# A fused attention and GEGLU block on one core: GpSimd's queue given out by a modelled clock, tangents, differences and projections held for smaller counted backlogs of ScalarE, no filler matmuls in three-tile steps

## The chip, the cores and the metric

The kernel runs on one core of one Trainium2 chip. The metric is the device time of one execution in microseconds. The core has TensorE (PE), VectorE (DVE), ScalarE (ACT), GpSimd (POOL) and SyncE (SP, which here only issues DMAs). Each engine takes its own instructions in order; they wait for each other with semaphores.

## The reference

The input x has 2048 rows of 512 values (bfloat16). The block is a pre-norm transformer layer with 32 heads of 16 values and a gated FFN of 1792 hidden values:

```python
h  = x + A(layernorm(x))      # A: qkv = x @ wqkv; 32 heads, Dh = 16; softmax(q k^T / 4) v; @ wo
h2 = h + B(layernorm(h))      # B: (gelu_tanh(x @ w_gate) * (x @ w_up)) @ w_down
```

## The kernel before

**Units and steps.** The attention is cut into 64 units: eight groups of 256 rows, and in each group eight slots of four heads. A unit is 16 steps, p0 to p15, so the program counts 1024 steps ("ticks"). In a step, two passes run side by side. Pass 1 (`p1_pair`, L825) computes the scores of 128 rows against 512 keys for two heads into two PSUM banks, and VectorE takes their row maxima in one instruction (L840). When a unit's maxima are there, GpSimd combines them to the negative row maximum, split into three bfloat16 parts (L868 to L876), a DMA transposes them (STG), and GpSimd adds them to three spare rows of Q (L888, function `add`), so that the scores of pass 2 come out with the maximum already subtracted. Pass 2 follows 24 steps behind: two tiles a step, each of two matmuls (L904) into one of four rotating banks and one exponential on ScalarE (L933) into a ring of probability tiles. At p7 to p10 of the unit after next, the PV matmuls (L947, sixteen a step) use those tiles; the result is evicted to OB at p10 (L669), transposed by DMA, and normalised by GpSimd (L981, a power of -1, and L985).

**Joint units.** In eleven units (`JOINT`: 12, 14, 17, 20, 25, 28, 33, 36, 41, 44, 49) one step's pair of scores is left out: ScalarE writes two *differences* of scores beforehand (`item_diff`, L1027, after GpSimd has negated a part of Q, L1014), and VectorE takes one combined maximum per head (L837, two instructions instead of one L840). Step p14 of such a unit is skipped; pass 2 makes up its two tiles in p15 of that unit and p1 of the next, which then have three tiles (`more`). The run has 1013 executed steps.

**The dense stream.** The remaining work is a queue of items that `Dense.piece` starts between the steps: Q, K and V projections in the first units; then for each group the output projection (`item_oproj`: L1087, L1091, eviction with row sums L1094, and two steps or more later the squares L1101, then the layer norm on GpSimd and a transposing DMA, hnT); the FFN's gate and up products (L1168), seven of each, with evictions to g_sb and u_sb (L669); and two down projections (`item_down`, L1220, L1225). Gelu is done in pieces: GpSimd computes the polynomial (L1158, L1159, L1160), ScalarE the tangent (L1148), GpSimd the rest (L1156, L1157) and the product with the up half (L1212, GUT). An item uses two buffers in turn, so a gate waits for the product of the one before the last. The list `prio` (PV, output projections) comes ahead of `ready` (gate, up, down); `extra` holds the differences. A step in which no item ran gets two filler matmuls of 128x512 (`want`, `dummy`, L1380).

**Two counters order the work.** They are arithmetic of the program, not measurements:

- `act_lag` is ScalarE's counted backlog. Each step it gains 0.478 for each exponential and loses 1.135 (never under 0); each eviction adds 0.48, a tangent 0.54, the OB eviction 0.27. A tangent may be issued (`later` in `gelu_chain`) when the count, plus 0.48 if a gate or up item is running, is at most `LAG_TH + SLOPE * n`, n being the steps it has waited, and the polynomial's end by the GpSimd clock is at most 1.3 us after the step's start. A gate or up item starts at 0.3 or less, a square is issued at 0.2 or less.
- `PoolStream` gives out GpSimd's work. `budget` gains 1.19 a step up to 1.25; an operation is issued when the budget reaches its cost (at most 1.0); the power L981 (`inv`) is kept out of p1 to p3 and p12 to p15. Beside it `pool.t` is a modelled time of GpSimd's queue (`charge`), with 1.135 us to a step.

Of the kernel before, what the change touches and what calls it, by code (L numbers as in the profile page):

```python
# [219 lines left out]
NPT_M, NPT_E, NPT_G = 23, 4, 7  # L220
NPT = NPT_M + NPT_E + NPT_G
PV_T = (15, 16, 17, 18)
ADDX = 3
LAGX = 8
PAUSE = 1
DOUBLES = 20
# [2 lines left out]
LAG_START = 0.3  # L229
LAG_OP = 0.2  # L230
TANH_LAG = 2
SLOPE = 0.02
JOINT = (12, 14, 17, 20, 25, 28, 33, 36, 41, 44, 49)
J_AT, J_GONE = 10, 14
LAG_EXTRA = 0.3
POLY = 1.3
TICK = 1.135
TOOK = {1.04: 1.13, 0.62: 0.7, 1.27: 1.26, 1.45: 1.67, 0.31: 0.4}
LAG_TH = 0.2


def bass_sequential_preLN__mha_block__geglu_ffn__prompt_kernel(nc, A_x, A_wqkv, A_wo, B_x, B_w_gate, B_w_up, B_w_down, out):
    dbg = None
    with ExitStack() as es:
# [97 lines left out]
        NU = len(units)  # L342
# [161 lines left out]
        class Banks:  # L504
            def __init__(self):
                self.free = [4, 5, 6, 7]
# [17 lines left out]
        class Dense:  # L524
# [12 lines left out]
            def add(self, genfn, *a, front=False, est=2, not_before=0):  # L537
                (self.prio if front else self.ready).append((genfn, a, est, not_before))
            def tick(self, now):
                self.now = now  # L540
                if self.pause > 0:
                    self.pause -= 1
# [9 lines left out]
            def piece(self):  # L552
                if self.single and self.pause > 0:
                    return 0
                while True:
                    if self.gen is None:
                        lim = 10 ** 9
                        for it in self.prio:
                            lim = min(lim, max(it[3], self.now))
                        self.prio.sort(key=lambda it: it[3])  # L560
                        if self.extra and self.now >= 16 * self.extra[0][1][0] + 2:
                            self._start(self.extra.pop(0))
                        elif self.prio and (not self.single or self.prio[0][3] <= self.now):
                            self._start(self.prio.pop(0))
                        elif self.extra and not tight() and act_lag[0] <= LAG_EXTRA and self.now + 2 <= lim and not (self.ready and self.ready[0][0] is item_up):
                            self._start(self.extra.pop(0))
                        elif self.ready and (not self.single or ((act_lag[0] <= (-1 if tight() else LAG_START) or force[0] or self.ready[0][0] not in (item_gate, item_up)) and startable(self.ready[0], lim - self.now) and self.ready[0][3] <= self.now and self.now + self.ready[0][2] + PAUSE - 1 <= lim)):
                            self._start(self.ready.pop(0))
                        else:
                            return 0  # L570
                    try:
                        cost = next(self.gen)
                        if isinstance(cost, tuple):
                            if self.single:
                                self.pause = cost[1]
                            if ticking[0]:
                                return 0
                            continue
                        return cost
                    except StopIteration as fin:  # L580
                        self.gen = None
                        self.done += 1
                        if self.single:
                            banks.give(self.bank)
                            self.pause = 0 if dve_free[0] else PAUSE
                        return fin.value
# [6 lines left out]
        dense = Dense()  # L593
        behind = [0]
        def tight():
            return dense.now // 16 in JOINT and dense.now % 16 >= J_GONE - 2 or bool(behind[0])

        deferred = []
        def defer(k, fn):
            deferred.append((dense.now + k, fn))  # L600
# [16 lines left out]
        class PoolStream:  # L617

            def __init__(self):
                self.q = []  # L620
                self.budget = 0.0
                self.t = 0.0
            def add(self, ops, then=None):
                for i, (cost, fn) in enumerate(ops):
                    self.q.append((cost, fn, then if i == len(ops) - 1 else None))
                if force[0] or not ticking[0]:
                    self.run(True)
            def spend(self, cost):
                self.budget -= cost
            def charge(self, took, ready=0.0):  # L630
                self.t = max(self.t, TICK * dense.now, ready) + took
                return self.t
            def run(self, flush=False):
                while self.q and (flush or self.budget >= min(self.q[0][0], 1.0) or (self.q[0][1].__name__ == 'inv' and dense.now % 16 == 0)):
                    if not flush and self.q[0][1].__name__ == 'inv' and dense.now % 16 in (1, 2, 3, 12, 13, 14, 15):
                        break
                    cost, fn, then = self.q.pop(0)
                    self.budget -= cost
                    self.charge(TOOK.get(cost, cost))
                    fn()  # L640
                    if then is not None:
                        then()
            def tick(self):
                self.budget = min(self.budget + 1.19, 1.25)
                self.run()
        ticking = [False]
        pool = PoolStream()

        act_lag = [0.0]
# [228 lines left out]
        def negm_post(ui):  # L878
            gi, slot = units[ui]
            c, hf = gi // 2, gi % 2  # L880
            par = ui % 2
            P.dma("sp", lambda e: e.dma_start_transpose(out=STG[:, par, :].rearrange("p (q s) -> p q s", q=2), in_=ST[:, par].rearrange("p q s -> p (q s)")),
                  ("stT", par), reads=[("ST", par)], writes=[("STG", par)])
            q_ap = QT[:, c, slot, 256 * hf:256 * hf + 256]
            def add():
                pool.spend(0.7)
                pool.charge(0.63, st_end[0] + 2.75)
                P.op("pool", lambda e: e.tensor_tensor(out=q_ap, in0=q_ap, in1=STG[:, par, :], op=ALU.add), reads=[("STG", par), ("qT", slot, c, hf)], writes=[("qT", slot, c, hf)])  # L888
                q_ready.add(ui)
            defer(ADDX + (ui == NU - 1), add)  # L890
        q_ready = set()
# [165 lines left out]
        def load_xres(gi):  # L1057
            assert gi < 2 or ffn_done.get(gi - 2), "dense stream too far behind (residual reuse)"
            for k in range(2):
                P.dma("sp", lambda e, k=k: e.dma_start(out=g_h(gi, k), in_=xv[:, 2 * gi + k, :]), ("xres", gi % 2, k), writes=[("h", gi % 2, k)])  # L1060

        otok_consumed = {}
        def post_onT(gi, k):
            gp = gi % 2
            if k == 0:
                load_xres(gi)
            P.dma("sp", lambda e: e.dma_start_transpose(out=OnT[:, k, :, :], in_=Otok[:, k, :]),
                  ("onT", k), reads=[("Otok", s_) for s_ in range(NSLOT)], writes=[("OH", k)])
            if k == 1:
                otok_consumed[gi] = True  # L1070
            dense.add(item_oproj, gi, k, front=True, est=3, not_before=dense.now + 5)

        hn_left = {}
        ffn_done = {}
# [60 lines left out]
        def gelu_chain(par, dE):  # L1135
# [4 lines left out]
            def later(n):  # L1140
                if not force[0] and tight():
                    defer(1, lambda: later(n))
                    return
                if not force[0] and (act_lag[0] + (0.48 if dense.gen is not None and dense.cur in (item_gate, item_up) else 0) > LAG_TH + SLOPE * n or poly_end[par] > TICK * dense.now + POLY):
                    defer(1, lambda: later(n + 1))
# [4 lines left out]
            def poly_done():  # L1150
                poly_end[par] = pool.t
                defer(TANH_LAG, lambda: later(0))
            def second():
# [229 lines left out]
        st_end = [0.0]  # L1383
        def unit_end(ui):
            pool.spend(1.8)
            st_end[0] = pool.charge(2.0, TICK * (16 * ui + 15) + 2.35)
            negm_pre(ui)
            negm_post(ui)

        p2_started = False  # L1390
        p1_next = []
        early_target = dense.done
        tick = 0
        J_ = sorted(JOINT)
        J_PREP = {max(160, 16 * (J_[i - 1] if i else 0) + 12): J_[i] for i in range(len(J_))}
        ticking[0] = True
        def next_tile():
            n = 2 * t2 - behind[0]
# [4 lines left out]
        while True:  # L1403
# [14 lines left out]
            more = 1 if behind[0] and tick % 2 else 0  # L1418
# [12 lines left out]
            act_tick(2 * p2_ok + more)  # L1431
            if p1_ok and tick in J_PREP:
                joint_prep(J_PREP[tick])
            gp1 = tick % 2
# [42 lines left out]
            if doubles[0]:  # L1477
# [3 lines left out]
                cost = 2  # L1481
            else:
                cost = dense.piece()
# [2 lines left out]
            for fn_ in early.get(tick, ()):  # L1486
                fn_()
            if p1_ok:
                want = 2
            elif tick % 2 == 0:  # L1490
                want, alone = 0, cost or 0
            else:
                want = max(0, FILL_2 - alone)
# [45 lines left out]
```

## Time and profile before

| what | value |
|---|---|
| three timed runs | 1234.58 to 1235.58 us, median 1235.29 |
| profiled execution | 1234.76 us, its span 1232.9 us |
| granted TensorE clock | 1.00 |
| first and last maximum (L840) start | 14.7 and 1179.3 us |
| L840, L933 | 1002 maxima of 1213 ns; 2000 exponentials, about 717 ns |
| fillers (L1380) | 697 matmuls |
| tangents (L1148) | 49, first at 246.5, last at 1182.8 us |

The rows of maxima overlap in part: each lasts 1.21 us, the next one starts 1.13 us after it when nothing is late. In the same way an exponential is shown with 0.72 us or more, and the next follows 0.48 us later. In the timeline, instructions of one line that follow each other closely are merged into one row with a count; the number in square brackets is the time that the engine stood idle before it, with what released it. The stages, as busy microseconds of each 100:

| window | PE | DVE | ACT | POOL |
|---|---|---|---|---|
| 100 to 200 | 85.0 | 100.0 | 98.3 | 69.1 |
| 500 to 600 | 92.1 | 98.8 | 99.95 | 63.5 |
| 800 to 900 | 91.3 | 98.9 | 99.9 | 70.2 |
| 1000 to 1100 | 87.8 | 99.7 | 98.9 | 57.9 |

After the last maximum, from about 1181 to 1204 us, ScalarE works off the exponentials that pass 2 is behind; from there to the end TensorE does the last group's output projection and FFN.

### The profile page before, as it was taken

What the parts mean: (1) busy time and instruction counts of PE and PEld (TensorE: products, weight loads), DVE (VectorE), ACT (ScalarE), POOL (GpSimd) and SP (SyncE); (2) the same over time, 40 slices, a digit from 0 to 9 for tenths busy, and PEclk for the clock granted to TensorE, in tenths of its full rate; (3) what the DMA queues carried; (4) which work ended last, traced back from release to release, by engine and by line L of the source; (5) the groups of instructions that cost most, each with busy time, mean ns of one, the idle gap of its engine ahead of it and who ended that gap; (6) DMA issues with size and microseconds to landing.
All of it is one profiled execution on the core that took longest, in us unless ns stands there. A gap on an engine that the chain in (4) does not pass through costs nothing.

```text
span 1232.9 us, 31298 instructions
## 1 busy us (share of the span) xinstructions
PE 1102.3 (89%) x12444; PEld 427.4 (35%) x12580; DVE 1179.1 (96%) x1107; ACT 1195.2 (97%) x2437; POOL 784.4 (64%) x1624
## 2 busy tenths in 40 slices
PE   7898888899999988999889998899889898888898
PEld 3233222233333333333333343333333333233335
DVE  8999999999999999999999999999999999999933
ACT  7899999999999999999999999999999999999993
POOL 8567873566756587466755677366765687347850
PEclk9999999999999999999999999999999999999999
DMA  5111113200011000100011000110001000100000
GB/s 152 27 34 30 33 50 116 76 10 9 8 27 25 8 10 9 39 13 8 11 25 27 8 8 11 25 27 8 9 10 38 14 9 8 35 17 10 8 19 14
DMA packets 68657, 31.53 MB, mean 26 GB/s; under 512 B 53920, under 2 KB 67488, under 8 KB 68512
## 3 DMA queue, kind: packets, MB, share of 16 engines
q1 hardware_dynamic: 68512, 29.52, 9.5%
q8 instruction: 101, 1.65, 0.6%
q14 instruction: 44, 0.36, 0.1%
HBM read 11.80 MB, written 2.10 MB: 11 GB/s over the span
## 4 chain that ended last, share of the span: by engine, by line
ACT 50%; DVE 30%; POOL 8%; PE 7%; issue 3%; DMA 1%; POOLq 0%; DVEq 0%
DVE PM L840 29%; ACT PTM L933 29%; ACT PTG L933 8%; ACT PTE L933 4%; PE pbank L1220 2%; ACT g_sb L669 1%; POOL th_sb L1158 1%; PE pbank L904 1%; ACT u_sb L669 1%; DMA STG<-ST 1%; PE pbank L825 1%; ACT th_sb L1148 1%; POOL LINV L981 1%; PE pbank L1168 1%; POOL GUT L1212 1%
## 5 line engine op out<-in xcount | busy, mean ns | idle before, releaser
L840 DVE TENSOR_REDUCE PM<-pbank 128x2 f32<-128x1024 f32 x1002 | 1141.4, 1213 | 8.8 <-PE pbank L904 5.1
L933 ACT ACTIVATE PTM<-pbank 128x512 bf16<-128x512 f32 x1357 | 730.3, 718 | 3.4 <-PE pbank L904 0.6
L904 PE MATMUL pbank<-QT,KT 32*128 32x256 bf16 x4096 | 512.2, 273 | 16.2 <-ACT PTM L933 6.0
L825 PE MATMUL pbank<-KT,QT 32*128 32x512 bf16 x2026 | 390.1, 384 | 29.9 <-DVE PM L840 11.3
L1380 PE MATMUL pbank<-ones_bf,ident 128*128 128x512 bf16 x697 | 217.3, 383 | 56.2 <-ACT PTM L933 29.1
L933 ACT ACTIVATE PTG<-pbank 128x512 bf16<-128x512 f32 x407 | 227.7, 716 | 1.2 <-PE pbank L904 0.2
L825 PEld LDWEIGHTS pbank<-KT,QT 32*128 32x128 bf16 x2026 | 97.7, 90 | 369.8 <-DVE PM L840 133.2
L904 PEld LDWEIGHTS pbank<-QT,KT 32*128 32x128 bf16 x4096 | 171.2, 92 | 85.2 <-ACT PTM L933 46.5
L933 ACT ACTIVATE PTE<-pbank 128x512 bf16<-128x512 f32 x236 | 139.1, 718 | 0.8
L947 PE MATMUL pbank<-PTM,VA 128*17 128x256 bf16 x2776 | 125.4, 274 | 1.5
L981 POOL TENSOR_TENSOR LINV<-OBT,negone 128x8 f32<-128x8 bf16 x62 | 103.4, 1668 | 0.0
L1380 PEld LDWEIGHTS pbank<-ones_bf,ident 128*128 128x128 bf16 x796 | 46.0, 97 | 140.1 <-ACT PTM L933 90.0
L1158 POOL TENSOR_TENSOR th_sb<-g_sb 128x512 f32<-128x512 f32 x49 | 50.9, 1040 | 41.6 <-ACT g_sb L669 41.6
L947 PEld LDWEIGHTS pbank<-PTM,VA 128*17 128x17 bf16 x2776 | 60.0, 89 | 45.7 <-issue 29.6
L1168 PE MATMUL pbank<-hnT_l,wg_sb 128*128 128x256 bf16 x448 | 67.0, 275 | 3.6
L1168 PE MATMUL pbank<-hnT_l,wu_sb 128*128 128x256 bf16 x448 | 67.1, 275 | 2.3
L868 POOL TENSOR_TENSOR MX<-PM,MX 128x8 f32<-128x8 f32 x64 | 12.8, 200 | 86.6 <-DVE PM L840 86.3
L1160 POOL TENSOR_TENSOR th_sb<-th_sb,g_sb 128x512 f32<-128x512 f32 x49 | 62.1, 1267 | 3.4
L1212 POOL TENSOR_TENSOR GUT<-th_sb,u_sb 128x512 bf16<-128x512 f32 x49 | 61.8, 1267 | 2.5
L1157 POOL TENSOR_TENSOR th_sb<-th_sb,g_sb 128x512 f32<-128x512 f32 x49 | 62.2, 1269 | 1.4
L888 POOL TENSOR_TENSOR QT<-QT,STG 128x256 bf16<-128x256 bf16 x64 | 42.7, 668 | 30.5 <-DMA STG<-ST 30.5
L1220 PE MATMUL pbank<-wd_sb,GUT 128*128 128x512 bf16 x210 | 57.3, 382 | 3.4 <-ACT OB L669 1.3
(163 smaller groups left out, 1096.0 us busy)
## 6 DMA issues: line engine op xcount, KB each, us to landing
QKS<-QKS SPq DMA_DIRECT2D x27, 112.0 KB, 2.1
x_sb<-in_A_x_dram SPq DMA_DIRECT2D x4, 512.0 KB, 5.5
xres<-in_A_x_dram SPq DMA_DIRECT2D x16, 128.0 KB, 2.3
out_dram<-out_sb SPq DMA_DIRECT2D x16, 128.0 KB, 1.7
wg_sb<-in_B_w_gate_dram SPq DMA_DIRECT2D x4, 448.0 KB, 3.6
wu_sb<-in_B_w_up_dram SPq DMA_DIRECT2D x4, 448.0 KB, 3.9
wd_sb<-in_B_w_down_dram SPq DMA_DIRECT2D x3, 512.0 KB, 4.2
STG<-ST SPq DMA_TRANSPOSE x64, 2.3
```

The source lines that it names most:

```text
L825: P.op("pe", lambda e, g=g, b=b: e.matmul(pbank[:, b, :], QT[32 * g:32 * g + 32, c, slot, 128 * qt:128 * qt + 128], KT[32 * g:32 * g + 32, ...
L840: P.op("dve", lambda e: e.tensor_reduce(out=PM[:, par, qt, kc, g:g + 2], in_=pbank[:, b:b + 2, :], axis=AX.X, op=ALU.max), reads=[("pb", b ...
L904: P.op("pe", lambda e, kt=kt, i=i: e.matmul(pbank[:, b, 256 * i:256 * i + 256], KT[32 * g:32 * g + 32, slot, 128 * kt:128 * kt + 128], QT[ ...
L933: P.op("act", lambda e, b=b, pi=pi: e.activation(out=PTt(pi), in_=pbank[:, b, :], func=ACT.Exp), reads=[("pb", b)], writes=[("PT", pi)], e ...
L947: P.op("pe", lambda e, g=g, kt=kt, pi=pi, i=i: e.matmul(pbank[32 * g:32 * g + 17, b, 0:256], VA[:, kt, 4 * slot + g, :], PTt(pi)[:, 256 * ...
L981: P.op("pool", lambda e: e.tensor_tensor(out=li, in0=o4[:, :, :, 16], in1=negone[:, 0:8].rearrange("p (q h) -> p q h", q=2), op=ALU.pow), ...
L1157: o(1.27, lambda e: e.tensor_tensor(out=ts_, in0=ts_, in1=gs, op=ALU.mult), [("th", par), ("g", par)])], then=done)
L1158: pool.add([o(1.04, lambda e: e.tensor_tensor(out=ts_, in0=gs, in1=gs, op=ALU.mult), [("g", par)], dE), o(0.62, lambda e: e.tensor_scalar( ...
L1168: P.op("pe", lambda e, dc=dc, fc=fc, i=i: e.matmul(pbank[:, b, 256 * i:256 * i + 256], w[:, dc, 128 * fc:128 * fc + 128], hT[:, dc, :], st ...
L1212: P.op("pool", lambda e: e.tensor_tensor(out=o_ap, in0=shp(ts_), in1=shp(us), op=ALU.mult), reads=[("th", par), ("u", par)], writes=o_keys ...
L1220: P.op("pe", lambda e: e.matmul(pbank[:, b, :], GUT[:, fc, 128 * k:128 * k + 128], wd_sb[:, fc, :], start=first, stop=last), reads=[("GUT" ...
L1380: P.op("pe", lambda e: e.matmul(pbank[:, b, :], ident[:], ones_bf[:, 0:512], start=True, stop=True), reads=["ident", "ones_bf"], writes=[( ...
```

## The change

It does these things:

- `PoolStream.run` no longer uses the budget. The new `fits` issues an operation when its start by the clock is at most 0.8 us (`AHEAD`) after the end of the present step, and when it doesn't run more than 0.3 us (`OVER`) past one of two due times that it would start before: the combination of maxima at the unit's end, and the addition to Q while that is outstanding (`add_due`).
- The addition to Q is put into the queue four steps after the unit's end instead of three (`ADDX`).
- Tangents: `LAG_TH` 0.05 instead of 0.2.
- Output projections: one that is due waits, for at most six steps, while the count is over 0.1, and the dense stream waits with it; the second of a group is due one step later.
- Differences: outside the last six steps before their unit they start at a count of 0.05 instead of 0.3. The first unit's preparation is at step 60 instead of 160.
- No filler in steps with three tiles.

```diff
-ADDX = 3
+ADDX = 4
+AHEAD, OVER = 0.8, 0.3
-LAG_TH = 0.2
+LAG_TH = .05
...
                         if self.extra and self.now >= 16 * self.extra[0][1][0] + 2:
                             self._start(self.extra.pop(0))
+                        elif self.prio and self.prio[0][0] is item_oproj and self.prio[0][3] <= self.now < self.prio[0][3] + 6 and act_lag[0] > 0.1:
+                            return 0
...
-                        elif self.extra and not tight() and act_lag[0] <= LAG_EXTRA and self.now + 2 <= lim and not (self.ready and self.ready[0][0] is item_up):
+                        elif self.extra and not tight() and act_lag[0] <= (LAG_EXTRA if self.now >= 16 * self.extra[0][1][0] - 6 else 0.05) and self.now + 2 <= lim and not (self.ready and self.ready[0][0] is item_up):
...
+            def fits(self, took):
+                t0 = max(self.t, TICK * dense.now)
+                if t0 > TICK * (dense.now + 1) + AHEAD:
+                    return False
+                due = [TICK * (dense.now // 16 * 16 + 15) + 2.35 if dense.now < 16 * NU else 1e9]
+                if self.add_due:
+                    due.append(st_end[0] + 2.75)
+                return not any(t0 < d < t0 + took - OVER for d in due)
             def run(self, flush=False):
-                while self.q and (flush or self.budget >= min(self.q[0][0], 1.0) or (self.q[0][1].__name__ == 'inv' and dense.now % 16 == 0)):
-                    if not flush and self.q[0][1].__name__ == 'inv' and dense.now % 16 in (1, 2, 3, 12, 13, 14, 15):
-                        break
+                while self.q and (flush or self.fits(TOOK.get(self.q[0][0], self.q[0][0]))):
                     cost, fn, then = self.q.pop(0)
-                    self.budget -= cost
                     self.charge(TOOK.get(cost, cost))
...
                 pool.charge(0.63, st_end[0] + 2.75)
+                pool.add_due = False
...
-            dense.add(item_oproj, gi, k, front=True, est=3, not_before=dense.now + 5)
+            dense.add(item_oproj, gi, k, front=True, est=3, not_before=dense.now + 5 + k)
...
             negm_post(ui)
+            pool.add_due = True
...
-        J_PREP = {max(160, 16 * (J_[i - 1] if i else 0) + 12): J_[i] for i in range(len(J_))}
+        J_PREP = {max(60, 16 * (J_[i - 1] if i else 0) + 12): J_[i] for i in range(len(J_))}
...
-                want = 2
+                want = 0 if more else 2
```

More of the change, by code (lines that the diff above doesn't have):

```diff
@@ L622, in __init__ @@
                 self.t = 0.0
+                self.add_due = False
             def add(self, ops, then=None):
@@ L643, in tick @@
             def tick(self):
-                self.budget = min(self.budget + 1.19, 1.25)
                 self.run()
```

## The prediction

> **What bounds the kernel now.** I read the page first, then the busy time by stage, then the timelines of the places where VectorE stood.
>
> ```profile
> span 1232.9 us, 31298 instructions
> ...
> PE 1102.3 (89%) x12444; PEld 427.4 (35%) x12580; DVE 1179.1 (96%) x1107; ACT 1195.2 (97%) x2437; POOL 784.4 (64%) x1624
> ...
> ACT 50%; DVE 30%; POOL 8%; PE 7%; issue 3%; DMA 1%; POOLq 0%; DVEq 0%
> ...
> L840 DVE TENSOR_REDUCE PM<-pbank 128x2 f32<-128x1024 f32 x1002 | 1141.4, 1213 | 8.8 <-PE pbank L904 5.1
> ```
>
> The profiled execution took 1234.76 us (span 1232.9), 0.5 under the median of the three timed runs, 1235.29; differences are taken from the profile and subtracted from the median. Two engines are full at once. A step of the main loop has one maximum (L840), and undisturbed maxima follow each other every 1.131 us (a row of n of them lasts n x 1.131 + 0.08). The first begins at 14.67, the last of 1013 steps at 1179.27. 1012 intervals of 1.131 are 1144.6, eleven joint steps add 0.087 each, so about 19 us were lost to waiting: 5.5 in units 0 to 2 (loads, V evictions, which the change leaves alone), nothing in units 3 to 10, and the rest later. **This rest, 13.6 us, is all that the main loop can give.** From the starts of the maxima, one by one, it falls into: 5.65 after a tangent near the PV steps; 4.46 around output projections and their squares; 1.58 at the three-tile steps; 0.33 elsewhere; 1.6 in excesses under 0.04 each, jitter. After the last maximum ScalarE works off 24 steps of exponentials (to 1203.7) and the last FFN follows (to 1232.9); no gain there.
>
> A tangent's case, unit 39, engines ACT, PE, DVE of the timeline (start, length, operation):
>
> ```profile
> 732.63 0.90 ACT L669 ACTIVATE u_sb<-pbank 128x512 f32<-128x512 f32 x1
> ...
> 734.06 0.95 ACT L1148 ACTIVATE th_sb<-th_sb 128x512 f32<-128x512 f32 x1
> ```
> ```profile
> 735.56 0.39 PE L904 MATMUL pbank<-QT,KT 32*128 32x256 bf16 x2 [0.55 <-ACT PTE L933]
> ```
> ```profile
> 729.58 6.87 DVE L840 TENSOR_REDUCE PM<-pbank 128x2 f32<-128x1024 f32 x6
> 736.86 2.35 DVE L840 TENSOR_REDUCE PM<-pbank 128x2 f32<-128x1024 f32 x2 [0.41 <-PE pbank L904]
> ```
>
> An eviction and a tangent within 1.5 us put ScalarE a whole operation behind; the score tile finds no free bank, TensorE stands 0.55, the next pair of scores is late, VectorE loses 0.41. The same tangent in unit 20, one step later in the unit and with nothing behind it:
>
> ```profile
> 392.07 0.84 ACT L1148 ACTIVATE th_sb<-th_sb 128x512 f32<-128x512 f32 x1
> ```
> ```profile
> 389.31 4.60 DVE L840 TENSOR_REDUCE PM<-pbank 128x2 f32<-128x1024 f32 x4
> ```
>
> 4 x 1.131 + 0.08 = 4.60: no loss. That pair is the core of my forecast.
>
> **Tangents (LAG_TH 0.2 to 0.05).** The code's count falls 0.179 a step: after an eviction 0.48, 0.30, 0.12, 0. Following the count through the old program, 39 of 49 tangents started above the new limit (0.05 + 0.02 per step waited); they are held one step, a few two. Of the 20 at p7, 17 stood at 0.12 or 0.16 with at most four steps waited: they go to p8 with 0, the harmless case; their stalls sum to 2.5 us. Three (units 24, 54, 62) had waited six steps: unchanged, 1.0 stays. Four at p6 of units 17, 31, 39, 47 stood at 0.30 and cost 0.49 each; held to p7 they stand at 0.12 like unit 38's, which cost 0.295: 4 x 0.2 = 0.8 gained. Held ones at p0 give 0.3, unit 22's 0.1. Sum 3.7, from 0 (the stalls move) to 5.9. Behind a tangent on ScalarE wait the exponentials; behind its two GpSimd operations (0.62, 1.27) the product for GUT. Between the last GUT product of a FFN and its first down projection lie 13 to 24 steps in the middle of the run, so a step late costs nothing there.
>
> **Output projections** (limit 0.1, the second one step later). Old: both evictions 2 steps apart, then both squares and a down eviction within four steps. The accumulator reads (0.09 each) are not in the count.
>
> ```profile
> 939.67 8.32 DVE L840 TENSOR_REDUCE PM<-pbank 128x2 f32<-128x1024 f32 x7
> 948.20 2.35 DVE L840 TENSOR_REDUCE PM<-pbank 128x2 f32<-128x1024 f32 x2 [0.20 <-PE pbank L904]
> 950.71 2.36 DVE L840 TENSOR_REDUCE PM<-pbank 128x2 f32<-128x1024 f32 x2 [0.16 <-PE pbank L904]
> ```
>
> 7 maxima should take 8.00: 0.32 lost inside, then more, 0.8 per group of heads. New: the first projection starts as before (the count is 0.09), its square comes before the second projection, which waits until the count is 0.07, some four steps later. The stall at the second eviction stays in part, the chain of four is broken up. I take half of 4.46, 2.2; bounds 0 and 4.4. The held projection also blocks the down item behind it; that then no longer fits before PV and goes about eight steps later, inside the spare steps. Its DMAs (the OnT transposes) leave at their old step; the hnT transposes move by a few steps on SP's queue, where DMA is at 1 or 2 tenths. Differences under 0.05 and the first preparation 100 steps earlier: no stall of the old run belongs to a difference except the 0.39 in unit 11, counted above. The first two move into units 4 to 10, where VectorE lost nothing; at worst each costs one eviction there, 2 x 0.48. I take nothing.
>
> **Fillers in the 22 three-tile steps.** TensorE:
>
> ```profile
> 687.41 0.39 PE L825 MATMUL pbank<-KT,QT 32*128 32x512 bf16 x2
> 687.64 0.60 PE L904 MATMUL pbank<-QT,KT 32*128 32x256 bf16 x6
> 688.35 0.60 PE L1380 MATMUL pbank<-ones_bf,ident 128*128 128x512 bf16 x2
> 688.88 0.39 PE L825 MATMUL pbank<-KT,QT 32*128 32x512 bf16 x2
> ```
>
> The step is 1.47 long (687.41 to 688.88), 0.34 over VectorE's; without 688.35 to 688.88 it is about 0.95. Two such steps outrun the spare of the score banks: 1.58 over the run, nearly all of it goes: 1.4. Floor 0, where the third exponential (3 x 0.478 = 1.43 in a step) is what ends last.
>
> The granted clock is 1.00 in every stage, and the gap that a missing filler leaves is under 0.2 us. [...]
>
> **GpSimd's clock.** GpSimd is 64% busy, and no other engine's wait list names it in the main loop, so its new order is worth nothing by itself. What it can do is harm. The addition (L888, 0.67) goes one step later; it ended 1.2 to 4.0 us before the unit's first score tile, and in 40 of 64 cases it waited for the transpose anyway (30.5 us in all). The rule lets nothing overrun its slot by more than 0.3, so it stays in time: 0. Polynomials (1.13, 0.70, 1.26) may now be issued in one step where three were used, so a tangent can follow sooner; between the end of L1160 and the start of L1148 there were 0.66 to 1.34 us in 15 pairs of 49 and over 3.3 in the others. I charge 1.3 for waits of this sort and for items that fall badly after the shifts (bounds 0 and 13, the rival below).
>
> **Sum:** 3.7 + 2.2 + 1.4 - 1.3 = 6.0 us; 1235.3 - 6.0 = **1229.3**. The tail: the last GUT product ended at 1189.3, its down projection began at 1194.4; 5 us cover one or two steps' delay.
>
> **Rivals.**
> - The stalls move. ScalarE's extra work is not reduced, only placed: if held tangents meet the OB eviction at p10 and later gates, the old loss returns elsewhere. For it: ScalarE is over 99% busy from 300 to 900. Against: unit 20. Only the fillers pay, 1.4 less 1: about 1235. Chance 0.18.
> - Slower: the tangent waits for GpSimd. The clock starts a polynomial when it is issued, though the gate's eviction ends about 1.6 us later (the first operations mostly started 1.3 to 3.1 after their step, and waited 41.6 us for g_sb in all). A tangent may be issued with 1.3 us of polynomial outstanding and starts 0.7 to 1.2 after its step: up to 0.6, plus up to 0.46 by which GpSimd already ran behind its clock, say 0.9. ScalarE takes its work in order and stands, all exponentials with it. A tangent that waits has no gain of its own, so the 3.7 goes: with ten of the 15 close pairs it is 9.0 less the 3.6 of projections and fillers, 1240.7; with all 15, 1245. It decides from four waits on (3.6 against 3.6). Against: the up item holds most tangents for three more steps. Chance 0.16.
> - The tail: if the last FFN slips more than five steps, its down projection (15 matmuls of 0.213, 3.2 us) falls behind the exponentials: 1232.5. Chance 0.07.
> - TensorE's clock drops at the three-tile steps: with matmuls twice as long, 0.95 of work becomes 1.9, 0.77 over VectorE's step, 22 times: 17, so 1246. [...] Chance 0.01; every clock row is 1.00.
>
> **Chances.** The forecast, 1225 to 1232.5, holds 0.58. About 0.2% (2.5 us) is what a measurement can tell from no change: faster (under 1232.8) 0.64 with most of the tail case, same 0.20, slower 0.16. The low end, 1224, is all 12 us of stalls gone; the high end, 1240, takes in the slower rival with ten waits. That leaves out 0.08 above and 0.05 below.
>
> **What would show it.** Right: tangents at p8 instead of p7 and no gaps of 0.3 before L840 at p9; no excess at p15 and p1 after joint units; L1101 of the first row before L1094 of the second; maxima from 14.7 to about 1173. Wrong: waits of ACT th_sb for POOL L1160; new gaps at p10 to p12; GUT's last product after 1190; a clock under 1.00.

## The result, and the profile after

The changed kernel is slower: a median of 1246.93 us (1245.04 to 1248.51, four runs) against 1235.01 (1234.58 to 1235.58, four runs) for the kernel before in the same comparison. The ratio is 1.0096, 95% interval 1.0081 to 1.0111. The forecast was 1229.3 with a range of 1224 to 1240. The profiled execution took 1245.8 us.

From the page of the changed kernel: the span, busy time by engine, the clock in 40 slices, the shares of the chain that ended last, and the maxima (L848; the lines of the main loop stand 8 later than before up to the combination of maxima and 9 later from the addition to Q on).

```profile
span 1244.1 us, 31391 instructions
...
PE 1135.4 (91%) x12544; PEld 428.3 (34%) x12544; DVE 1180.3 (95%) x1107; ACT 1196.0 (96%) x2437; POOL 784.9 (63%) x1624
...
PEclk9999999998999999999999999999999999999999
...
ACT 61%; DVE 21%; PE 13%; issue 3%; DMA 1%; POOL 1%; SPq 0%; POOLq 0%; DVEq 0%
...
L848 DVE TENSOR_REDUCE PM<-pbank 128x2 f32<-128x1024 f32 x1002 | 1142.8, 1214 | 19.1 <-PE pbank L913 14.9
```

The engines do the same work as before, except for the fillers: 36 fewer of them, 760 by their weight loads after 796. (Each matmul has a weight load of its own, 12544 of each above. The trace of before has 12444 matmuls beside 12580 weight loads: it lacks the records of 136, 99 of them fillers, and the 697 in the table ahead of the prediction are too few. So TensorE isn't 33 us busier, as the two pages read. With each missing matmul put in at its weight load, its busy time is 1131.7 us before and 1135.4 after.) TensorE's share of the chain rises from 7% to 13%, and VectorE's idle time before the maxima from 8.8 to 19.1 us, most of it ended by score matmuls of pass 2 (L913, 14.9). One slice of the clock row shows an 8, nothing else does: a slice is 31 us, and what happened lasts 3.4.

The first maximum starts at 14.69 (before 14.67), the last at 1190.42 (before 1179.27), and from there to the end it is 53.7 us in both. All 11.15 us are lost between the maxima. Sorted by place, from their starts one by one (us lost beyond 1.131 a step):

| place | before | after | difference |
|---|---|---|---|
| units 0 to 2 | 5.47 | 6.52 | +1.05 |
| p7 to p10 | 6.34 | 7.46 | +1.12 |
| three-tile steps | 1.58 | 0 | -1.58 |
| other stalls | 4.06 | 4.03 | -0.03 |
| at a halved TensorE clock | 0 | 10.46 | +10.46 |
| joint steps and jitter | 2.58 | 2.70 | +0.12 |

(In the prediction, p7 to p10 and the others were split by cause, not by place.) So the stalls at the three-tile steps did go, and **the clock took their place**. Windows of the changed kernel behind unit 14 (length; busy time and count of PE, weight loads, VectorE, ScalarE, GpSimd; granted clock; DMA):

```profile
289.45:292.87 3.42, 2.99 (x28) 1.12 (x28) 3.42 (x4) 3.42 (x8) 0.97 (x6) 1.00 0.02 5
292.87:296.28 3.41, 3.41 (x16) 0.63 (x16) 2.82 (x3) 3.12 (x7) 2.83 (x6) 0.50 0.09 19
296.28:299.69 3.41, 3.41 (x27) 1.27 (x26) 2.83 (x3) 2.55 (x6) 0.37 (x1) 0.50 0.00 0
```

For 6.8 us the granted clock is 0.50. TensorE's timeline there:

```profile
289.69 0.60 PE L913 MATMUL pbank<-QT,KT 32*128 32x256 bf16 x6
290.52 0.39 PE L833 MATMUL pbank<-KT,QT 32*128 32x512 bf16 x2 [0.22 <-DVE PM L848]
...
291.93 0.82 PE L913 MATMUL pbank<-QT,KT 32*128 32x256 bf16 x6
...
293.88 1.03 PE L1389 MATMUL pbank<-ones_bf,ident 128*128 128x512 bf16 x2
294.84 0.61 PE L833 MATMUL pbank<-KT,QT 32*128 32x512 bf16 x2
...
296.35 0.61 PE L833 MATMUL pbank<-KT,QT 32*128 32x512 bf16 x2
```

The rows with x6 are the two three-tile steps, now without fillers; a filler pair then takes 1.03 us instead of 0.60, and a step 1.51 (294.84 to 296.35). VectorE waits in each of these steps; the first:

```profile
295.49 1.22 DVE L848 TENSOR_REDUCE PM<-pbank 128x2 f32<-128x1024 f32 x1 [0.59 <-PE pbank L913]
```

This happens behind eight of the eleven joint units (14, 25, 28, 33, 36, 41, 44, 49) and once in unit 58: ten stretches of 3.41 us in all. With half the clock missing for 34.1 of 1244.1 us, the mean over the run is 0.986, as the profile has it. Each stretch starts a whole number of 3.413 us after the others (292.9 to 494.3 is 59 of them).

Three smaller losses come from the other parts.

**Unit 1 and unit 16: late additions to Q.** GpSimd in units 0 and 1, then in unit 16, with TensorE's wait:

```profile
45.93 0.77 POOL L750 TENSOR_SCALAR KT<-QKS,kmask,kbias 128x512 bf16<-128x512 bf16 x1 [2.16 <-DMA QKS<-QKS]
46.66 0.67 POOL L897 TENSOR_TENSOR QT<-QT,STG 128x256 bf16<-128x256 bf16 x1
...
311.81 1.04 POOL L1167 TENSOR_TENSOR th_sb<-g_sb 128x512 f32<-128x512 f32 x1 [3.48 <-ACT g_sb L677]
...
320.16 0.67 POOL L897 TENSOR_TENSOR QT<-QT,STG 128x256 bf16<-128x256 bf16 x1 [1.74 <-DMA STG<-ST]
```
```profile
320.97 0.39 PE L833 MATMUL pbank<-KT,QT 32*128 32x512 bf16 x2 [1.21 <-POOL QT L897]
```

The clock issues an operation by a modelled length and doesn't know when its input comes. A K operation waited 2.16 us for its load with the addition behind it (1.27 us lost at p7 of unit 1). A polynomial waited 3.48 us for its gate ahead of the combination of maxima, which then ran 2 us late; its transpose landed 4.5 us after its issue (2.3 in that unit before), and 1.08 was lost. The spare between an addition's end and the first score tile was 1.16 us or more before; in some twenty units it is now under 0.52.

**Unit 58:** a down item went late, its eviction ended at 1086.36, and its output DMA waited for that on SP's queue with the OnT transposes behind it, whose data had been ready since 1078.37 (L994). Before, the transposes left within 0.3 us of their data. TensorE stood 2.10 us for OnT, VectorE lost 1.43, and the clock halved after it. (With the projections' edit alone, e6 below, the output DMA also stands ahead of the transposes, but it leaves at 1075.91 and nothing is lost in unit 58. So the held projections alone don't make this stall; what else of the change it takes stays open.) SP's queue and TensorE:

```profile
1086.38 0.33 SPq L1249 DMA_DIRECT2D out_dram<-out_sb  x1
1086.76 1.20 SPq L1076 DMA_TRANSPOSE OnT<-Otok  x1
```
```profile
1093.54 0.60 PE L1096 MATMUL pbank<-wo_sb,OnT 128*128 128x512 bf16 x2 [2.10 <-DMA OnT<-Otok]
```

### The profile page after: what moved, and what is told of

Same layout as the page of the kernel before. It is cut to its first block, busy times and chain, and to the rows that moved or that the text cites. A ratio compares the mean times of both kernels' runs of the same rounds, so it can differ in the third digit from the quotient of the medians.

```text
span 1244.1 us, 31391 instructions
## 1 busy us (share of the span) xinstructions
PE 1135.4 (91%) x12544; PEld 428.3 (34%) x12544; DVE 1180.3 (95%) x1107; ACT 1196.0 (96%) x2437; POOL 784.9 (63%) x1624
## 4 chain that ended last, share of the span: by engine, by line
ACT 61%; DVE 21%; PE 13%; issue 3%; DMA 1%; POOL 1%; SPq 0%; POOLq 0%; DVEq 0%
ACT PTM L942 35%; DVE PM L848 20%; ACT PTG L942 11%; ACT PTE L942 6%; PE pbank L1229 3%; PE pbank L833 2%; PE pbank L913 2%; ACT th_sb L1157 2%; ACT g_sb L677 2%; ACT u_sb L677 2%; PE pbank L1389 2%; PE pbank L1177 1%; ACT OB L677 1%; PE pbank L775 1%; PE pbank L440 1%
## 5 line engine op out<-in xcount | busy, mean ns | idle before, releaser
L848 DVE TENSOR_REDUCE PM<-pbank 128x2 f32<-128x1024 f32 x1002 | 1142.8, 1214 | 19.1 <-PE pbank L913 14.9
L913 PE MATMUL pbank<-QT,KT 32*128 32x256 bf16 x4096 | 517.0, 275 | 17.6 <-ACT PTM L942 8.4
L833 PE MATMUL pbank<-KT,QT 32*128 32x512 bf16 x2026 | 394.3, 387 | 34.9 <-DVE PM L848 14.9
L1389 PE MATMUL pbank<-ones_bf,ident 128*128 128x512 bf16 x760 | 234.0, 392 | 34.9 <-ACT PTM L942 8.8
L913 PEld LDWEIGHTS pbank<-QT,KT 32*128 32x128 bf16 x4096 | 172.4, 92 | 87.8 <-ACT PTM L942 49.0
L1177 PE MATMUL pbank<-hnT_l,wg_sb 128*128 128x256 bf16 x448 | 67.8, 277 | 3.7 <-ACT PTM L942 0.9
L1177 PE MATMUL pbank<-hnT_l,wu_sb 128*128 128x256 bf16 x448 | 67.3, 275 | 2.2
L1229 PE MATMUL pbank<-wd_sb,GUT 128*128 128x512 bf16 x224 | 63.8, 400 | 0.6 <-ACT PTM L942 0.2
L748 POOL TENSOR_SCALAR QT<-QKS,qmask 128x512 bf16<-128x512 bf16 x30 | 46.8, 1565 | 16.2 <-ACT QKS L677 16.2
```

Of the source, the lines that this page charges most:

```text
L833: P.op("pe", lambda e, g=g, b=b: e.matmul(pbank[:, b, :], QT[32 * g:32 * g + 32, c, slot, 128 * qt:128 * qt + 128], KT[32 * g:32 * g + 32, ...
L848: P.op("dve", lambda e: e.tensor_reduce(out=PM[:, par, qt, kc, g:g + 2], in_=pbank[:, b:b + 2, :], axis=AX.X, op=ALU.max), reads=[("pb", b ...
L913: P.op("pe", lambda e, kt=kt, i=i: e.matmul(pbank[:, b, 256 * i:256 * i + 256], KT[32 * g:32 * g + 32, slot, 128 * kt:128 * kt + 128], QT[ ...
L1177: P.op("pe", lambda e, dc=dc, fc=fc, i=i: e.matmul(pbank[:, b, 256 * i:256 * i + 256], w[:, dc, 128 * fc:128 * fc + 128], hT[:, dc, :], st ...
L1229: P.op("pe", lambda e: e.matmul(pbank[:, b, :], GUT[:, fc, 128 * k:128 * k + 128], wd_sb[:, fc, :], start=first, stop=last), reads=[("GUT" ...
L1389: P.op("pe", lambda e: e.matmul(pbank[:, b, :], ident[:], ones_bf[:, 0:512], start=True, stop=True), reads=["ident", "ones_bf"], writes=[( ...
```

## The experiments

Every time below is a median of ten or eleven runs (e2: four) beside the kernel before in the same comparison; brackets are 95% intervals of the ratio. "Lost" is the sum between maxima of the profiled run, 20.0 for the kernel before.

**The changed kernel with its fillers back (e1)**

```diff
-                want = 0 if more else 2
+                want = 2
```

> The changed kernel with one line undone: the two fillers stand in the three-tile steps again. Theory (the missing fillers let TensorE's clock halve after the joint units, and that is most of the loss): the eight half-clock stretches after joint units vanish; the main loop gives back about 9.6 us of the 10.5 lost in such stretches and pays 1.6 again for the fillers, about 1238.5 us; the stretch in unit 58, behind a projection that waited for its transpose, may stay. Rival (the loss is in the new places of GpSimd's and ScalarE's work, and the clock only follows stalls that are there anyway): the stretches stay in part and the time stays over 1243.

1236.39 against 1235.15, ratio 1.0012 [1.0002, 1.0021]: 10.5 of the 11.9 us are back, 2 more than the theory expected. The joint units no longer lower the clock. One stretch of 0.50 is left (380.1 to 383.5), behind two differences, which are 32-row matmuls in steps without a filler.

**The kernel before without those fillers (e2)**

```diff
-                want = 2
+                want = 0 if more else 2
```

> The kernel before with one line of the change: no filler in three-tile steps, all else as it was. Theory: half-clock stretches of 3.41 us after most of the eleven joint units, about 1.1 us of lost time each, less the 1.6 us that the fillers cost: about 1242 us, between 1240 and 1246. Rival: no stretch, TensorE being over 85% busy, and the 1.6 us are gained: 1233.5.

1246.46 against 1235.15, 1.0087 [1.0072, 1.0102]: this one line makes nearly the whole loss, 11.3 of 11.9 us. It is just over the upper bound expected, 1246, where single stretches were thought of: clock 0.982, 10.85 us lost at 0.50 in six places, up to 10.2 us long; the 1.58 of three-tile stalls are gone here too.

**One filler instead of two (e3), and two fillers of 32 columns (e4), in the kernel before**

```diff
-                want = 2
+                want = 1 if more else 2
```

> The kernel before with one filler instead of two in each three-tile step. If the clock asks for a share of work in a stretch, one filler per step (0.22 of 1.13 us) may be enough: clock 1.00 and 1234 to 1235. If it asks for as much as the two gave, stretches in some joint units, 1237 to 1242.

```diff
-                P.op("pe", lambda e: e.matmul(pbank[:, b, :], ident[:], ones_bf[:, 0:512], start=True, stop=True),
+                P.op("pe", lambda e: e.matmul(pbank[0:cols, b, :], ident[:, 0:cols], ones_bf[:, 0:512], start=True, stop=True),
...
-                dummy(..., want - (cost or 0))
+                dummy(..., want - (cost or 0), 32 if more else 128)
```

> The kernel before with both fillers in the three-tile steps, but 32 columns of the stationary matrix instead of 128: the same time on TensorE, a quarter of its array. If the clock follows the time in which TensorE is busy, nothing changes: clock 1.00, 1235. If it follows how much of the array works, the stretches come as without fillers, with the fillers' time still paid: about 1244.

e3: 1235.12 against 1235.15, 0.9999 [0.9990, 1.0009], clock 1.00 in the profiled execution (0.997 in one of the ten). The stalls of the three-tile steps fall from 1.58 to 0.29, but p7 to p10 rise from 6.34 to 7.22: with the clock held, the gain forecast for this step isn't there either. e4: 1234.73, 0.9997 [0.9988, 1.0007], clock 1.00 in all ten: a quarter of the columns holds the clock as well.

**Two fillers of 32 rows (e9)**, the quarter of the array the other way: 32 rows, 128 columns, 512 columns moving

```diff
+                    P.op("pe", lambda e: e.matmul(pbank[:, b, :], KT[32 * g:32 * g + 32, 0, 0:128], KT[32 * g:32 * g + 32, 0, 0:512], start=True, stop=True, tile_position=(32 * g, 0)),
...
-                dummy(..., want - (cost or 0))
+                dummy(..., want - (cost or 0), next_row() if more else None)
```

> The kernel before with both fillers in the three-tile steps, of the same length and with all 128 columns, but on 32 rows of the array instead of 128. The stretches in the two unfilled kernels began after a stretch of 3.41 us in which the sum of moving columns times active rows over 128 was 0.26 to 0.38 of the full rate; nearly all others lay over 0.38. If this sum decides, 32-row fillers count a quarter, about 0.06 more than none: stretches come, 1240 to 1247. If the mere time in which TensorE works decides, or the columns: clock 1.00, 1235.

1236.32 against 1234.84, 1.0018 [1.0007, 1.0029]: slower, but less than the 1240 to 1247 expected, and three of the ten executions kept 1.00. In the profiled execution, which was one of the longest (1239.91), the clock falls in three places, 5.46 us lost. The window ahead of the first fall (the next, from 494.12, is at 0.50); then a window of the changed kernel, in unit 16, behind which nothing fell:

```profile
490.71:494.12 3.41, 2.78 (x21) 0.99 (x20) 3.41 (x4) 3.41 (x8) 2.96 (x8) 1.00 0.11 24
```
```profile
320.17:323.59 3.42, 2.38 (x49) 1.11 (x49) 2.42 (x3) 2.54 (x6) 3.26 (x5) 1.00 0.00 0
```

TensorE was busier ahead of this fall (2.78, or 3.01 with a filler whose record is missing) and ahead of the one at 292.87 (2.99, longest gap 0.22) than where nothing fell (2.38, with a gap of 1.21). So it is neither busy time nor the length of a gap; e4 and e9 use the same area of the array for as many columns, and the clock kept 1.00 in ten of ten executions and in three of ten, so it is not area. **What separates them is rows.** Count each matmul as columns moved times the share of the 128 rows it uses; a full one of 512 columns repeats every 0.216 us at a clock of 1.00 (L1229 at 1238.33 of the changed kernel: twelve in 2.75, the last shown with 0.38), so a stretch of 3.413 holds about 16 of them (15.8). An ordinary step has two score matmuls (0.25 each), four tile matmuls (0.125 each) and two fillers (1 each): 3, so 9 in a stretch. The stretch from 289.45 above has 6 score matmuls, 16 tile matmuls and 2 fillers: 1.5 + 2 + 2 = 5.5.

The border is sharp when three things are taken care of. The traces of before, e5, e6, e7 and e9 lack 136 matmul records each; their weight loads are there and say where they belong. A matmul that runs across the edge of a stretch is shared out between the two. And four PV matmuls, which use 17 columns each, are counted once, by the time that they take: in e12

```profile
316.57 0.61 PE L965 MATMUL pbank<-PTM,VA 128*17 128x256 bf16 x16
```

sixteen of them take 0.61 us, as long as four up products with as many columns moved (L1177, 0.61 at 286.69 of the changed kernel). Counted so, the 24 stretches ahead of a fall in all sixteen profiles have 4.0 to 6.03, and the other 5351 stretches at 1.00, between 20 and 1178 us, have 6.00 or more; the kernel before has 6.7 or more. e9 has seven stretches from 6.0 to 6.3, two of which fell, so it stands on the border. Its fillers also move other data than those of e4 (K instead of ones); what speaks for rows is the count over all the runs, not e9 alone.

**Tangents alone (e5)** and the same with a filler beside each difference (e11), in the kernel before

```diff
-LAG_TH = 0.2
+LAG_TH = .05
```

> The kernel before with the tangents' limit alone (0.05 for 0.2). By the step of the prediction that counted 3.7 us of stalls: 1231.5, and the stalls at p8 and p9 behind tangents at p6 and p7 gone. Rival (held tangents meet the OB eviction and later gates, the stalls move): 1234 to 1236.

1236.11 against 1234.84, 1.0007 [0.9998, 1.0017]: the rival's time. At p7 to p10 the loss falls from 6.34 to 4.16, 2.2 of the 3.7 forecast. Elsewhere 0.56 at other steps, 0.41 at three-tile steps and 0.65 of jitter come back, and 1.18 in a stretch of half clock. TensorE ahead of it:

```profile
558.28 0.39 PE L1022 MATMUL pbank<-KT,QT 32*128 32x512 bf16 x1
...
560.73 0.38 PE L1022 MATMUL pbank<-KT,QT 32*128 32x512 bf16 x1
...
562.23 1.03 PE L1380 MATMUL pbank<-ones_bf,ident 128*128 128x512 bf16 x2
```

Two differences (L1022, each with L1024 behind it) have come within 2.5 us; their steps have no filler, and the next filler pair takes 1.03.

```diff
         (item_diff)
-            return 3
+            return 1
```

> The kernel before with the tangents' limit alone, and one filler beside each difference, whose two matmuls use 32 rows of the array and had stood in place of fillers. The tangents alone showed a half-clock stretch after a stretch with two differences (row sum 0.35 of the full rate) and 1.2 us lost in it. If the differences are the cause: clock 1.00, 1.2 us less than that run, about 1234.9. If not, the stretch stays and the time too, 1236.

1235.11 against 1234.99, 1.0006 [0.9998, 1.0015]. That stretch is gone, and the time is 1.0 less than in e5, near the 1.2 expected. The profiled execution, one of five near 1237 where the other six take 1235.1 or less, has another in unit 59, behind a wait of TensorE for hnT (1.69 us); it costs 1.89, with the stall of 1.34. The held tangents are worth nothing that can be measured.

**Projections alone (e6), and with one filler in three-tile steps (e10)**

```diff
+                        elif self.prio and self.prio[0][0] is item_oproj and self.prio[0][3] <= self.now < self.prio[0][3] + 6 and act_lag[0] > 0.1:
+                            return 0
...
-            dense.add(item_oproj, gi, k, front=True, est=3, not_before=dense.now + 5)
+            dense.add(item_oproj, gi, k, front=True, est=3, not_before=dense.now + 5 + k)
```

> The kernel before with the output projections' wait and later due step alone. By the prediction 2.2 us less: 1233. Rival (the held projection pushes the down item and its output DMA ahead of the next group's transposes, as in unit 58 of the changed kernel, where TensorE stood 2.1 us): some of the stalls go, one of 1.5 to 3 us comes in, with or without a half-clock stretch: 1234 to 1237.

> The kernel before with the projections' wait (2.4 us faster alone) and one filler instead of two in three-tile steps (same time alone, 1.3 us of stalls less at those steps in its trace). If both add up: 1231.3 and clock 1.00. Rival: the three-tile stalls move to p7 to p10, as in the single run: 1232.4.

e6: 1232.43 against 1234.84, 0.9980 [0.9970, 0.9989]. e10: 1232.16 against 1234.99, 0.9979 [0.9970, 0.9987]. VectorE in e6 over the same group of heads whose rows broke at 948 and 950 before:

```profile
928.13 30.85 DVE L842 TENSOR_REDUCE PM<-pbank 128x2 f32<-128x1024 f32 x27
```

27 x 1.131 + 0.08 = 30.62: 0.23 lost in all, and no gap. The other stalls fall from 4.06 to 0.55; p7 to p10 rise from 6.34 to 8.05, which takes back 1.7. Unit 58 loses nothing, so the rival's stall isn't there. In e10 p7 to p10 rise to 8.64: about half of what the one filler takes off the three-tile steps moves there, and the time is nearer to the rival's 1232.4.

**GpSimd's clock alone (e7), and only from step 64 on (e13)**

```diff
+            def may(self):
+                if dense.now >= 64:
+                    return self.fits(TOOK.get(self.q[0][0], self.q[0][0]))
...
-                while self.q and (flush or self.fits(TOOK.get(self.q[0][0], self.q[0][0]))):
+                while self.q and (flush or self.may()):
...
-            defer(ADDX + (ui == NU - 1), add)
+            defer(ADDX - (ui < 4) + (ui == NU - 1), add)
```

(The diff is e13's against e7; e7 has the change's `fits`, `add_due` and `ADDX` and nothing else of it; below step 64 `may` is the old budget.)

> The kernel before with GpSimd's clock and the later addition alone. Theory (the clock gives out polynomials whose input is not there yet; the combination of maxima queues behind them and the addition to Q ends just before, or after, the unit's first score tile): spare between addition and tile under 0.5 us in a third of the units, one stall of about 1.2 us in unit 1, one or two more of about 1: 1236 to 1239. Rival (the lost spare costs nothing): 1235 or less.

> The kernel before with GpSimd's clock and the later addition, but from step 64 on only. With the clock from the start, one stall of 1.74 us in unit 1 (the addition queued behind a K operation that waited for its DMA) stood against 2.3 us gained elsewhere. Theory: the stall goes, 1232.7. Rival: the stall in unit 1 is from the V evictions that came earlier, or the gains were by chance: 1234.4 or more.

e7: 1234.37 against 1234.84, 0.9997 [0.9988, 1.0007]. e13: 1233.31 against 1234.99, 0.9986 [0.9977, 0.9995]. In e7 unit 1 loses 1.74 at p7 (1.27 in the changed kernel); in e13 it doesn't. e7 is faster than its theory had it: the spare did shrink (under 0.52 us in 16 units), but only this one stall came. So the clock gains some 1.7 where inputs are early, and gives most of it back in one unit where a load is late.

**The change mended (e12):** the changed kernel with one filler in three-tile steps, one beside each difference, and e13's rule

> The changed kernel with three things mended: one filler in three-tile steps, one beside each difference, GpSimd's old rule and the addition after three steps in the first four units. If the clock, the differences and the late addition in unit 1 are the causes of the loss: no half-clock stretch but perhaps unit 58's, 1246.9 less 10.5 (fillers), 1.2 (stretch behind differences), 1.2 (unit 1), 0.5: about 1233.5, under the kernel before. If something else is left in the change, 1236 or more.

1234.31 against 1234.99, 0.9995 [0.9987, 1.0004]. The losses of unit 1 and of the joint units are gone; in unit 16 the addition is still late (1.48 lost), and the clock falls with it (2.26 in all). With these three mended the change is worth nothing that can be measured.

**What gained, together (e14), and the tangents on top (e15):** the kernel before with e6's, e13's and e3's edits; then `LAG_TH` 0.05 as well

> The kernel before with the output projections' wait and the second projection a step later, GpSimd's clock from step 64 on, and one filler in three-tile steps; tangents and differences as before. The first alone took 2.4 us off, the second 1.7. Theory A (each removes stalls of its own, so they add up): 1230.9, bounds 1230.4 to 1231.4, and under 15.5 us lost between first and last maximum. Theory B (both draw on the same stalls, ScalarE's work being only placed anew): 1232 to 1233, no better than the projections alone, about 17.7 us lost. Either way a granted clock of 1.00; a half-clock stretch would add 1.2 to 2.3 and say that a unit's waits fell on a step with few matmuls.

> The same with the tangents' limit of 0.05 as well; differences as before. Theory A (a held tangent gains at its place, 2.2 us of stalls at p7 to p10 in the run of tangents alone, once nothing else disturbs): 1228.7 to 1230, under the kernel without the limit by 1 to 2. Theory B (the held tangents push the up and down items behind them into worse steps, which took back the 2.2 in the run of tangents alone): no better than without the limit, 0 to 2.5 slower, with stalls at p11 to p15 in place of those at p7 to p10.

e14: 1232.85 against 1235.17, 0.9985 [0.9976, 0.9993]; e15: 1234.76, 1.0001 [0.9992, 1.0010]. Theory B has the time right in both. e14 loses 17.5 us in all, as e10 does (17.5), e6 (17.7) and e13 (17.9); with 8.26 at p7 to p10. Projections and clock draw on the same stalls. In e15 the tangents take 0.37 off p7 to p10, and two falls of the clock (493.5 and 783.6, the first behind a three-tile step with one filler and a difference with none) cost 2.62; the stalls at p11 to p15 that theory B named for e15 didn't come. The best measured is e10, 2.8 us under the kernel before; e6, e13 and e14 stand within 1.2 of it.

## Why the prediction was wrong, step by step

- **"Fillers in the 22 three-tile steps" is the step that failed.** It forecast that of 1.58 us "nearly all of it goes: 1.4". It went, and 10.46 came in its place; e1 and e2 show this from both sides. The other terms failed beside it: they were to give 3.7 + 2.2 - 1.3 = 4.6, and with the fillers back (e1) the rest of the change costs 1.2. The prediction set the drop of the clock aside because "the granted clock is 1.00 in every stage, and the gap that a missing filler leaves is under 0.2 us". Both were true or nearly so (the longest gap in the stretch from 289.45 is 0.22), and neither bears on it. The clock was 1.00 in the trace of before with the fillers in it; a row in which the cause is present can't price its absence. And in the runs it is not the gaps that set the stretches ahead of a fall apart from the others, but rows times columns: 5.5 of 16 there, with the border at 6.0. With the clock held (e3), this step gains nothing, since the stalls move to p7 to p10.
- **The rival of the clock** was given 1246 and a chance of 0.01. The end fits, its parts do not: it took 22 single steps at 0.77, 17 us, off a forecast of 1229.3; what happened is ten stretches of about 1.05, and almost no gain from the rest. That matmuls take twice as long was its assumption, which no run had shown then; the changed kernel shows it: a full one repeats every 0.427 us where the granted clock is 0.50 (L1229 from 549.05, three in 1.46) and every 0.216 where it is 1.00. It counted the steps that would suffer, and the falls go by stretches, a whole number of 3.413 us apart. Neither busy time nor a gap tells which: one came after a stretch of 2.99 of 3.42 us busy and a longest gap of 0.22, and none after one of 2.38 busy with a gap of 1.21.
- **Projections**: 2.2 forecast, 2.4 measured (e6). Right in size, partly by luck: by place it is 3.5 gained, 0.4 more at the three-tile steps, and about 1.7 given back, where the prediction halved 4.46 without saying where the rest would go. In the changed kernel it doesn't show, since unit 58 and three stalls of 0.36 at p11 (units 34, 42, 50) stand in the same row of the table. The prediction let the blocked down item go "inside the spare steps", and named SP's queue for the hnT transposes only; the item's output DMA on that queue is what held OnT in unit 58 of the changed kernel (not in e6).
- **Tangents**: 3.7 forecast. 2.2 of it came at the place forecast (e5), and nothing was left of it in the time (+1.3, interval across no change). The rival "The stalls move" names this, and e14 against e10 and e6 shows it for the projections and the clock as well: where ScalarE is over 99% busy, an order that removed a stall in one step made another in each of these runs.
- **GpSimd's clock**: charged 1.3, with a wait of tangents for polynomials as the mechanism. No tangent (L1157) waits in the changed kernel. (Nor was GpSimd quite absent from the other engines' waits before: TensorE stood 0.7 us once for QN, L1014.) The harm is of the kind that the step called nothing: "The rule lets nothing overrun its slot by more than 0.3, so it stays in time: 0". The slot is kept only by a model in which inputs are there.
- **Differences**: taken at nothing. They cost something by the same count as the fillers: behind two within 2.5 us the clock fell in e1 and e5, and with a filler beside each (e11) that fall is gone.
- **The tail** came as forecast: 53.7 us after the last maximum. (A matmul of its down projection repeats every 0.216 us in the traces, where the prediction has 0.213; fifteen take 3.2 either way.)

What stays open: whether the border of 6 of 16 holds for other kernels, what besides the projections makes the stall of unit 58, and how safe the kernel before is. Of 110 executions of it that were timed beside the experiments, 26 show a clock of 0.999, about one stretch, and all of these take over 1235.1 us; no trace of them was kept, so where it lies isn't known.

## What to carry to other kernels

A filler can be the reason why the clock row reads 1.00 (a mean of 0.982 without these, e2); before one is taken away, add up what TensorE does without it in every stretch of 3.4 us, weighing each matmul by the rows it uses (in these runs 6 of 16 full ones in 3.413 us were the border; for another kernel that is not shown), and thin it (one instead of two as in e3, or fewer columns as in e4) rather than drop it. A queue that is given out by a model must be told when inputs arrive, or one late load puts everything behind it past its due time (2.16 us of waiting and 1.27 lost in unit 1). Where an engine is over 99% busy, price a removed stall at what the whole run gains from it alone, not at its own length.

## What the runs showed of the hardware that was not expected

- TensorE's granted clock fell to 0.50 even after a stretch in which TensorE was busy for 2.99 of 3.42 us and idle for at most 0.22 us at a time. It went with rows times columns moved per 3.413 us: all 24 falls came behind 4.0 to 6.03 of 16 full matmuls, and of the other 5351 stretches at 1.00, between 20 and 1178 us, none had under 6.00. Fillers of 128 rows and 32 columns held it in all ten executions (e4), fillers of 32 rows and 128 columns in three of ten (e9).
- Sixteen PV matmuls of 17 columns took 0.61 us, as long as four of 128 columns (L1177) with as many columns moved; the border above is found with four of them counted once.
- A fall lasted one to three of these stretches (3.4 to 10.2 us), and a stretch cost 0.8 to 1.0 us (10.46 in ten after the change, 10.85 in thirteen in e2).
- A transposing DMA of the same form (STG) landed 4.5 us after its issue in unit 16 of the changed kernel, where the kernel before had it after 2.3; over the whole run before, the longest was 3.9.
